# Reordering the head and the late plan of a fused spectral filter and MLP kernel on one Trainium2 core

## The chip, the cores and the metric

The kernel runs on one core of one Trainium2 chip. The metric is the device time of one execution in microseconds (us). For a ratio, the mean time of one kernel's fast runs is divided by the mean time of the other's fast runs of the same rounds, so a ratio is not quite the ratio of the medians that I quote. All runs gave correct results, and all were fast, that is within 1.5% of the fastest run of their kernel, but for one run of the kernel before (614.06 us), which the ratios leave out. The runs were made on at least three chips, and each set of rounds had the kernel before beside it: so ratios are the safer comparison between runs of different rounds. One execution per kernel carries a profile; it can differ from the median by some microseconds, and positions in time ("at 63.68") are microseconds from the start of that profiled execution.

The engines are called by the profile's names: PE is the tensor engine (PEld its weight loads), DVE is VectorE, ACT is ScalarE, POOL is GpSimd, SP is the sync engine; a trailing q means the instruction queue that issues transfers (SPq).

## The reference

```python
X = np.fft.rfft(x, axis=1)                 # x: 8 batches x 3136 tokens x 256
y = np.fft.irfft(X * (filt_r + 1j * filt_i)[None], n=3136, axis=1)
h = y.transpose(0, 2, 1) @ U @ V           # rank 32 along the tokens
u = y + h.transpose(0, 2, 1)
out = u + np.maximum(u @ w_ch1, 0.0) @ w_ch2
```

## The kernel before

3136 is 64 x 49, and the transform is done as matrix products in four stages. Stage 1 transforms 64 points (tile `a` before its trip through DRAM is `asb`), stage 2 transforms 49 points and is followed by the filter product on DVE or POOL (`ta`, `tb`, `y`, or `uv` for batch 0), stage 3 goes back over 49 points (`esb`), stage 4 back over 64 (`ut`). Between stages 1 and 2, and between 3 and 4, the data go out to DRAM (`ct`) and come back in another order: as `a` for stage 2 and as `e` for stage 4. Batch 0 avoids the first trip: its stage 1 is computed already "turned", and PE transposes bring it into order.

The rank-32 part is folded into stage 4. Its 96 contraction rows are 64 rows of `e` plus 32 "H rows" in `e[64:96]`, the same for each residue; the weights' rows `sv[64:96]` hold V. Then come the two MLP products, `mm1` with ReLU and `mm2`. The order of everything is written by hand. One "step" is one eighth of a group of 512 tokens; a batch has 48 to 52 steps of about 1.25 us.

```python
# batch 0: stage 2, filter product, stage 3
turn_a2(0); turn_a2(1)
for j in range(16):
    ...                                     # stage 2 of half tile j into pz
    if j % 5 in (1, 3):                     # product on POOL, from a copy by ACT
        nc.scalar.copy(pc, pz)
        nc.gpsimd.tensor_mul(uv, pc, fin)
    else:                                   # product on DVE
        nc.vector.tensor_mul(uv, pz, fin)
    if half and k + 2 < 8:
        turn_a2(k + 2)                      # 8 transposes, 98 columns each
    if j in (4, 6, 8, 10):
        load_x(1, j // 2 - 2)
    ...                                     # stage 3 and esb copy, four behind

# from batch 0 to the MLP
mid_first()
nc.gpsimd.tensor_copy(sv[64:96, :]..., vnat...)          # V into sv, on POOL
for c in range(3):
    load_e2(0, c)
load_e2(0, 6)
low_rank(0); low_rank_end(0)
for c in (0, 1, 2, 6):
    put_h(0, c)                 # nc.sync.dma_start(t[64:96], h1 ...)
stage4(groups[0], 0); stage4(groups[0], 1)

# the late plan (batches 1 to 7), in steps
lead = 5 if b > 1 else 2        # stage-2 loads ahead of the stage-2 matmul
s = later(s, 1)                 # spacing of stage 2 after a product on DVE
plan_st1(b, later(start[b - 1], -55))                    # stage 1, b > 2
m = later(start[b - 1], -8) if b > 1 else 10             # stage 2
```

A filler group without work (`Group(None, 7)`) stands between batches 0 and 1 and pads the plan there.

## Time and profile before

| | before |
|---|---|
| median of three runs | 607.46 us (605.84 to 607.73) |
| profiled execution | 599.7 us |
| last stage-3 matmul of batch 0 ends | 49.34 |
| first stage-4 matmul of batch 0 | 63.68 |
| first stage-2 matmul of batch 1 | 92.34 |
| first stage-4 matmul of batch 1 | 151.81 |
| from there to the end | 447.89 us |

The positions are read from the timeline, which lists what each engine did in order of time (start, duration, line, what was issued; times count). They cut the program into stretches. This is the sync engine's own timeline of the kernel before, at one of the later changes from batch to batch (start, duration, line, what was issued; times count):

```profile
400.95 0.54 SPq L317 DMA_DIRECT2D ct<-esb  x1
407.05 0.48 SPq L418 DMA_DIRECT2D e<-ct  x1
...
408.27 0.65 SPq L424 DMA_DIRECT2D e<-h  x1
...
409.62 1.43 SPq L308 DMA_DIRECT2D a<-ct  x3
```

The last write of `ct` is issued at 400.95. The load of `e` that reads it can be issued only when it has landed, at 407.05. The three loads of `a` for the next batch do not depend on that write, but they stand behind it in the same queue and go out at 409.62. PE reached the stage-2 matmul before they had landed and waited 2.83 us (the matmul starts at 412.58).

### The profile page before, as it was taken

The page shows a single profiled execution, that of the slowest core. Times are in us where ns is not written, and L with a number is a line of the kernel's source. Part 1 is how long each engine was busy: PE and PEld are TensorE (multiplying, and loading weights), DVE is VectorE, ACT ScalarE, POOL GpSimd, SP SyncE. Part 2 cuts the span into 40 slices and gives each one's busy share as a digit, 9 for nine tenths or more (in the row PEclk, how much of TensorE's full clock was granted, in tenths as well). Part 3 has the DMA queues.
Part 4 walks back from the last instruction along what each step waited for, and adds up shares of the span by engine and source line. Part 5 has one row for each costly group of instructions (what it writes and reads, how often), then busy time and mean ns, then how long its engine had stood idle before and what let it go on. Part 6 is the DMA issues. An engine that isn't in the chain of part 4 may idle for free.

```text
span 599.7 us, 11562 instructions
## 1 busy us (share of the span) xinstructions
PE 525.0 (88%) x4467; PEld 383.4 (64%) x4467; DVE 332.2 (55%) x384; ACT 379.8 (63%) x676; POOL 266.5 (44%) x171
## 2 busy tenths in 40 slices
PE   3992468996799869998999979998999999999997
PEld 2761245674567647775777757775777766777775
DVE  6661645672464646672676357744666367733332
ACT  7362244885377737884786747884886667766663
POOL 4776004992187306860486218830684048600000
PEclk9997677999799999999999989998999999999999
DMA  9997355878447784696558766597364654353212
GB/s 204 145 185 177 54 127 109 241 170 243 118 121 216 156 218 122 184 210 186 151 172 200 171 177 193 148 243 190 117 181 142 173 162 140 100 166 107 89 64 87
DMA packets 82598, 95.32 MB, mean 159 GB/s; under 512 B 6853, under 2 KB 63640, under 8 KB 82544
## 3 DMA queue, kind: packets, MB, share of 16 engines
q1 hardware_dynamic: 74736, 78.40, 45.0%
q0 software_dynamic: 7360, 15.91, 16.3%
q8 instruction: 35, 0.57, 0.4%
q10 hardware_dynamic: 448, 0.28, 0.2%
q14 instruction: 19, 0.16, 0.1%
HBM read 57.42 MB, written 49.77 MB: 179 GB/s over the span
## 4 chain that ended last, share of the span: by engine, by line
PE 54%; DVE 8%; ACT 3%; DMA 3%; issue 2%; SPq 2%; DVEq 0%; ACTq 0%
PE psum L471 19%; PE psum L504 19%; PE psum L340 3%; PE psum L460 3%; PE psum L480 3%; PE psum L332 3%; DVE tb L600 2%; DVE tb L598 2%; DMA a<-ct 2%; PE psum L254 2%; DVE och L512 1%; DVE ta L596 1%; PE psum L396 1%; ACT asb L261 1%; SPq L424 1%
## 5 line engine op out<-in xcount | busy, mean ns | idle before, releaser
L475 ACT ACTIVATE hring<-psum 128x512 f16<-128x512 f32 (+1 forms) x416 | 238.2, 576 | 160.7 <-PE psum L471 158.7
L471 PE MATMUL psum<-ut,w1sb 128*128 128x512 f16 (+1 forms) x832 | 243.6, 375 | 0.5 <-DVE ut L465 0.4
L504 PE MATMUL psum<-w2sb,hring 128*128 128x256 f16 x1536 | 233.7, 276 | 0.0
L602 POOL TENSOR_TENSOR y<-ta,tb 128x1024 f16<-128x1024 f16 x56 | 118.8, 2128 | 221.5 <-DVE tb L600 216.5
L504 PEld LDWEIGHTS <-hring 128*128 128x128 f16 x1536 | 145.1, 99 | 62.3 <-issue 1.9
L465 DVE CAST ut<-psum 128x512 f16<-128x512 f32 x96 | 71.0, 740 | 150.0 <-PE psum L460 135.5
L471 PEld LDWEIGHTS <-w1sb 128*128 128x128 f16 x832 | 103.2, 145 | 22.7 <-issue 6.2
L512 DVE COPY och<-psum 128x512 f32<-128x512 f32 x96 | 66.0, 688 | 50.6 <-PE psum L480 50.5
L314 ACT CAST esb<-psum 98x512 f16<-98x512 f32 x128 | 75.1, 588 | 22.3 <-PE psum L332 17.6
L596 DVE TENSOR_TENSOR ta<-psum,fb 128x1024 f16<-128x1024 f32 x41 | 50.1, 1221 | 35.3 <-PE psum L340 32.0
L460 PEld LDWEIGHTS <-e 96*128 96x128 f16 x768 | 36.8, 100 | 42.6 <-issue 24.0
L340 PE MATMUL psum<-a,w2t 98*128 98x512 f16 x135 | 43.0, 400 | 22.9 <-DMA a<-ct 16.5
L460 PE MATMUL psum<-sv,e 96*128 96x64 f16 x768 | 39.9, 196 | 22.9 <-issue 12.6
L480 PE MATMUL psum<-idn,ut 128*128 128x128 f16 x392 | 54.6, 221 | 0.0
L261 ACT CAST asb<-psum 128x512 f16<-128x512 f32 x78 | 46.0, 591 | 9.3 <-PE psum L254 8.2
L598 DVE TENSOR_TENSOR tb<-psum,fc 64x1024 f16<-64x1024 f32 x41 | 50.2, 1226 | 1.0
L600 DVE TENSOR_TENSOR tb<-psum,fc 64x1024 f16<-64x1024 f32 x41 | 49.9, 1217 | 0.6
L332 PE MATMUL psum<-y,g 128*98 128x512 f16 x105 | 39.8, 379 | 2.7 <-ACT esb L314 1.5
L480 PEld LDWEIGHTS <-ut 128*128 128x128 f16 x392 | 38.9, 99 | 5.2
L254 PE MATMUL psum<-x,wf 128*128 128x256 f16 x168 | 32.4, 284 | 7.8 <-DVE asb L259 6.3
L340 PEld LDWEIGHTS <-w2t 98*128 98x128 f16 x135 | 13.7, 102 | 31.5 <-issue 26.5
L598 POOL TENSOR_TENSOR tb<-pc,fc 64x1024 f16<-64x1024 f16 x15 | 31.9, 2123 | 1.2
(81 smaller groups left out, 341.8 us busy)
## 6 DMA issues: line engine op xcount, KB each, us to landing
out_dram<-och SPq DMA_DIRECT2D x48, 512.0 KB
ct<-esb SPq DMA_DIRECT2D x64, 196.0 KB
x<-in_x_dram POOLq DMA_DIRECT2D x24, 512.0 KB, 7.9
e<-ct SPq DMA_DIRECT2D x48, 256.0 KB
a<-ct SPq DMA_DIRECT2D x56, 196.0 KB
ct<-asb SPq DMA_DIRECT2D x42, 256.0 KB
e<-h SPq DMA_DIRECT2D x24, 128.0 KB
wf<-wf SPq DMA_DIRECT2D x3, 256.0 KB
```

The source lines that it names most:

```text
L314: nc.scalar.copy(esb[b, k][:, 2 * half:2 * half + 2, :].rearrange("p s d -> p (s d)"), pe[0:98])
L340: nc.tensor.matmul(pz, w, a, start=True, stop=True)
L460: nc.tensor.matmul(pu[:, 64 * i:64 * i + 64], e2[b, c][:, i, 128 * dh:128 * dh + 128], sv[:, 64 * r:64 * r + 64], start=(i == 0), stop=Tru ...
L465: nc.vector.tensor_copy(o, v)
L471: nc.tensor.matmul(ph[:, 0:n], w1sb[:, dh, :, t], gr.ut[:, dh, 0:n], start=(dh == 0), stop=(dh == 1))
L475: nc.scalar.activation(h[:, 0:n], ph[:, 0:n], RELU)
L480: nc.tensor.matmul(o[:, dh * 128:dh * 128 + 128], gr.ut[:, dh, t0:t0 + n], idn, start=False, stop=(dh == 1), skip_group_check=True)
L504: nc.tensor.matmul(o, gr.h[tt][:, i * 128:(i + 1) * 128], w2sb[:, tt, :], start=(tt == 0), stop=False, skip_group_check=True)
L512: nc.vector.tensor_copy(gr.och[:, 2 * y:2 * y + 2, :].rearrange("p j d -> p (j d)"), gr.pc)
L598: eng.tensor_mul(tb[0:64], p[64:128], vb[64:128])
L600: eng.tensor_mul(tb[64:128], p[0:64], vb[0:64])
L602: nc.gpsimd.tensor_add(ys[k], ta, tb)
```

## The change

The intent is to shorten the serial head of the program, up to batch 1, and to take the waits for loads out of the later batches. The diff, cut to its core:

```diff
 # x in 2 KB pieces instead of 8 KB
-            t = sb.tile([128, 8, DM], F16, tag="x", bufs=4, name="x")
-            nc.gpsimd.dma_start(t, dram(x.tensor, ..., [[NR * DM, 64], [24 * DM, 2], [1, 8 * DM]]))
+            t = sb.tile([128, 4, XW], F16, tag="x", bufs=4, name="x")
+            for h in range(2):
+                nc.gpsimd.dma_start(t[h:128:2, :, 0:2 * DM],
+                                    dram(x.tensor, ..., [[NR * DM, 64], [2 * DM, 4], [1, 2 * DM]]))
 # batch 0: transposes of 128 columns, four turns ahead of the loop
-                    nc.tensor.transpose(z[0:98, ...], free(fc, 0, 128, ..., [[32, 98]]), idn)
+                    nc.tensor.transpose(z[:, ...], free(fc, 0, 128, ..., [[32, 128]]), idn)
-        turn_a2(0)
-        turn_a2(1)
+        for k in range(4):
+            turn_a2(k)
+        for c in range(4):
+            load_x(1, c)
-            if j % 5 in (1, 3):
+            if j in (4, 6, 9, 11, 14):
-            if half and k + 2 < 8:
-                turn_a2(k + 2)
-            if j in (4, 6, 8, 10):
-                load_x(1, j // 2 - 2)
+            if j < 4:
+                turn_a2(j + 4)
+            if j == 8:
+                nc.scalar.copy(sv[64:96, :]..., vnat...)
 # H rows by VectorE
-        nc.sync.dma_start(t[64:96], free(h1[b], 64, 96, 0, [[0, n], [1, DM]]))
+        nc.vector.tensor_copy(t[64:96], free(h1[b], 64, 96, 0, [[0, n], [1, DM]]))
 # no filler group
-        if b == 0:
-            groups.append(Group(None, 7))
 # from batch 0 to the MLP
     mid_first()
-    nc.gpsimd.tensor_copy(sv[64:96, :]..., vnat...)
-    for c in range(3):
-        load_e2(0, c)
-    load_e2(0, 6)
+    load_e2(0, 0)
+    make_fa(0)
     low_rank(0)
+    first = st1(1)              # 4 of 13 units of batch 1's stage 1
     low_rank_end(0)
+    ...                         # 4 more units, then the other loads of e
 # late plan
-        lead = 5 if b > 1 else 2
+        lead = (2, 6, 9)[min(b, 3) - 1]
-                s = later(s, 1)
+                s = later(s, 2 if b > 1 and k % 2 else 1)
-            plan_st1(b, 13, (0, 1, 3, 4, 7))             # b == 2
+            plan_st1(b, 10, (0, 1, 3, 4, 7))
-            plan_st1(b, later(start[b - 1], -55))        # b > 2
+            plan_st1(b, later(start[b - 1], -60))
-        m = later(start[b - 1], -8) if b > 1 else 10
+        m = later(start[b - 1], -9) if b > 1 else 5
 # batch 1's first stage 4, with no filler group before it, at the end of batch 0's last group
-            if n + 1 < len(groups) and t in (2, 6) and groups[n + 1].c < 7:
+            if n + 1 < len(groups) and t in ((2, 6) if n != 5 else (6, 7)):
```

Not shown: the four parts of batch 1's second filter (`make_fa`) and batch 2's x loads also come one to three steps earlier, and a piece of `fc` is set to zero (the wider transposes read it).

More of the change, by code (lines that the diff above doesn't have):

```diff
@@ L20 @@
 NB = 8
+XW = 2 * DM + 16
 ALPHA, BETA = 1.0 / 64, 1.0 / 49
@@ L141, in bank @@
     def bank(tag):
-        of = {"m": (0, 1), "o": (2, 3), "w": (4,), "e": (7,), "f": (0, 1, 2, 3, 4, 7), "e0": (7, 4), "w1": (7, 5, 6)}[tag]
+        of = {"m": (0, 1), "o": (2, 3), "w": (4,), "e": (7,), "f": (0, 1, 2, 3, 4, 7), "e0": (7, 4), "f0": (0, 1), "w1": (7, 5, 6)}[tag]
         turn[tag] = turn.get(tag, -1) + 1
@@ L163, in load_x @@
         else:
-            t = sb.tile([128, 8, DM], F16, tag="x", bufs=4, name="x")
-            nc.gpsimd.dma_start(t, dram(x.tensor, (b * SEQ + 8 * c) * DM,
-                                        [[NR * DM, 64], [24 * DM, 2], [1, 8 * DM]]))
+            t = sb.tile([128, 4, XW], F16, tag="x", bufs=4, name="x")
+            for h in range(2):
+                nc.gpsimd.dma_start(t[h:128:2, :, 0:2 * DM],
+                                    dram(x.tensor, (b * SEQ + 24 * h + 8 * c) * DM,
+                                         [[NR * DM, 64], [2 * DM, 4], [1, 2 * DM]]))
         xt[b, c] = t
@@ L196 @@
                    free(zero, 32, 64, 0, [[0, NK * DM // 64], [1, 64]]))
+    nc.vector.memset(fc[:, 24:29, :], 0.0)
     usb = hflat[0:64, 0:NR * RANK]
@@ L254, in st1 @@
                     nc.tensor.matmul(pf[:, i * DM:(i + 1) * DM], wf[:, 8 * c + 2 * j + i, :],
-                                     xt[b, c][:, 2 * j + i, :], start=(i == 0), stop=True,
+                                     xt[b, c][:, j, DM * i:DM * i + DM], start=(i == 0), stop=True,
                                      skip_group_check=True)
@@ L290, in turned @@
                         nc.tensor.matmul(z[:, 128 * i:128 * i + 128],
-                                         xt[0, c][:, g + i, 128 * hh:128 * hh + 128],
+                                         xt[0, c][:, (g + i) // 2, DM * (i % 2) + 128 * hh:DM * (i % 2) + 128 * hh + 128],
                                          wf[:, 8 * c + g + i, :], start=(i == 0), stop=True,
@@ L343, in mid_first @@
         a2 = {}
+        spare = [sb.tile([128, 2, 4 * DM], F16, tag="asb", bufs=3, name="asb") for _ in range(3)]
         def turn_a2(k):
-            z = bank("m").bitcast(F16)
+            z = bank("f0").bitcast(F16)
             for i in range(4):
                 for hh in range(2):
-                    nc.tensor.transpose(z[0:98, DM * i + 128 * hh:DM * i + 128 * hh + 128],
-                                        free(fc, 0, 128, 3136 * hh + 4 * k + i, [[32, 98]]), idn)
-            a2[k] = sb.tile([98, 4 * DM], F16, tag="a2", bufs=4, name="a2")
+                    nc.tensor.transpose(z[:, DM * i + 128 * hh:DM * i + 128 * hh + 128],
+                                        free(fc, 0, 128, 3136 * hh + 4 * k + i, [[32, 128]]), idn)
+            if k < 2:
+                a2[k] = sb.tile([98, 4 * DM], F16, tag="a2", bufs=4, name="a2")
+            else:
+                a2[k] = spare[k // 2 - 1][0:98, k % 2, :]
             nc.vector.tensor_copy(a2[k], z[0:98])
@@ L378, in mid_first @@
                 nc.vector.tensor_mul(uv, pz, fin)
-            if half and k + 2 < 8:
-                turn_a2(k + 2)
-            if j in (4, 6, 8, 10):
-                load_x(1, j // 2 - 2)
+            if j < 4:
+                turn_a2(j + 4)
+            if j == 8:
+                nc.scalar.copy(sv[64:96, :].rearrange("p (r q) -> p r q", q=NQ),
+                               vnat.rearrange("p (q r) -> p r q", q=64))
             todo.append((j, uv))
@@ L428, in __init__ @@
             self.b, self.c = b, c
-            self.ntok = {6: 128, 7: 256}.get(c, 512)
+            self.ntok = 512 if c < 6 else 128
             self.h = []
@@ L515, in mm2_part, with make_fa @@
                                        [[NR * DM, 64], [4 * DM, 2], [1, 4 * DM]]), gr.och)
+    fa = fb
+    def make_fa(i):
+        s = slice(8 * i, 8 * i + 8)
+        nc.vector.tensor_copy(fc[0:64, s], fb[64:128, s])
+        nc.vector.tensor_scalar_mul(fc[64:128, s], fb[64:128, s], -1.0)
+        nc.vector.tensor_copy(fa[64:128, s], fb[0:64, s])
+        if i == 3:
+            nc.vector.tensor_copy(fa[64:65, 31, :], fc[0:1, 31, :])
+            for p in (0, 64):
+                nc.vector.memset(fc[p:p + 1, 31, :], 0.0)
     u_hat()
@@ L523 @@
     mid_first()
-    nc.gpsimd.tensor_copy(sv[64:96, :].rearrange("p (r q) -> p r q", q=NQ),
-                          vnat.rearrange("p (q r) -> p r q", q=64))
-    for c in range(3):
-        load_e2(0, c)
+    load_e2(0, 0)
+    make_fa(0)
+    low_rank(0)
+    first = st1(1)
+    for _ in range(4):
+        next(first)
+    low_rank_end(0)
+    for _ in range(4):
+        next(first)
+    load_e2(0, 1)
+    load_e2(0, 2)
     load_e2(0, 6)
-    low_rank(0)
-    low_rank_end(0)
     for c in (0, 1, 2, 6):
@@ L551, in small @@
     def small(s):
-        return s // 8 < len(groups) and groups[s // 8].c >= 6
+        return s // 8 < len(groups) and groups[s // 8].c == 6
     def ok_dve(s):
@@ L564, in at @@
         plan[s].append((f, a))
-    fa = fb
-    def make_fa(i):
-        s = slice(8 * i, 8 * i + 8)
-        nc.vector.tensor_copy(fc[0:64, s], fb[64:128, s])
-        nc.vector.tensor_scalar_mul(fc[64:128, s], fb[64:128, s], -1.0)
-        nc.vector.tensor_copy(fa[64:128, s], fb[0:64, s])
-        if i == 3:
-            nc.vector.tensor_copy(fa[64:65, 31, :], fc[0:1, 31, :])
-            for p in (0, 64):
-                nc.vector.memset(fc[p:p + 1, 31, :], 0.0)
     def plan_mid(b, s, on_pool):
@@ L663, in plan_st1 @@
         return s
-    gens = {}
+    gens = {1: first}
     def step1(b):
@@ L673 @@
         at(8 * c - 14, load_e2, 0, c)
-    for i in range(4):
-        at(i, make_fa, i)
-    for u in range(13):
-        at(3 + u // 3, step1, 1)
+    for i in range(1, 4):
+        at(i - 1, make_fa, i)
+    for u in range(5):
+        at(u // 2, step1, 1)
     for c in range(4):
-        at(9 + 2 * c, load_x, 2, c)
+        at(6 + 2 * c, load_x, 2, c)
     for b in range(1, NB):
         if b == 2:
-            plan_st1(b, 13, (0, 1, 3, 4, 7))
+            plan_st1(b, 10, (0, 1, 3, 4, 7))
         elif b > 2:
-            plan_st1(b, later(start[b - 1], -55))
-        m = later(start[b - 1], -8) if b > 1 else 10
+            plan_st1(b, later(start[b - 1], -60))
+        m = later(start[b - 1], -9) if b > 1 else 5
         z = plan_mid(b, m, (2, 5) if b > 1 else (1, 3, 5))
@@ L693 @@
                 f(*a)
-            if gr.c < 7:
-                mm1(gr, t)
-            if n + 1 < len(groups) and t in (2, 6) and groups[n + 1].c < 7:
-                stage4(groups[n + 1], t // 4)
-            if n and groups[n - 1].c < 7:
+            mm1(gr, t)
+            if n + 1 < len(groups) and t in ((2, 6) if n != 5 else (6, 7)):
+                stage4(groups[n + 1], t // 4 if n != 5 else t - 6)
+            if n:
                 mm2_part(groups[n - 1], t)
```

## The prediction

The sum of 36.4 us is the estimate from times in the trace of the kernel before, such as the 184 and 104 ns of the weight loads, the 0.69 us of L570, the 2.5 us of the loads of `a` and the clock of 0.77.

> **What bounds the kernel now.** I read the page's busy shares and slices first, to see where the tensor engine (PE) is not full; then its waits; then the timeline at the longest.
>
> ```profile
> span 599.7 us, 11562 instructions
> PE 525.0 (88%) x4467; PEld 383.4 (64%) x4467; DVE 332.2 (55%) x384; ACT 379.8 (63%) x676; POOL 266.5 (44%) x171
> ...
> PE   3992468996799869998999979998999999999997
> ...
> PEclk9997677999799999999999989998999999999999
> ```
>
> PE is busy 525.0 of 599.7 us and no other engine passes 63%, so the kernel is PE work plus 74.7 us of PE holes plus a slower clock. A slice is 15 us: the holes sit in the first eleven slices, and there PEclk falls to 6 or 7 tenths. By stretches (the windows view, with the end of each hole from the timeline) the idle time is 10.4 us in 0-15, 1.2 in 15-45, 14.3 in 45-63.7, 22.3 in 63.7-165 and 26.5 after.
>
> The waits of PE, longest first:
>
> ```profile
> PE psum L340 <- DMA a<-ct: 16.5, 6, 5.5
> PE psum L460 <- issue: 12.6, 1, 12.6
> PE psum L236 <- DVE hring L231: 9.1, 1, 9.1
> PE psum L254 <- DVE asb L259: 6.3, 1, 6.3
> PE psum L340 <- DVE tb L600: 5.8, 11, 1.1
> PE psum L460 <- DMA e<-h: 5.4, 1, 5.4
> PE psum L460 <- DMA a<-ct: 3.1, 1, 3.1
> ```
>
> Columns are total us, number, longest. All but the third (start of the program) and the fifth (DVE product) are hand-overs from one stage to the next through DRAM, or DVE work in front of one. The one put down to "issue" is no issue cost. The timeline of 45.6 to 64 shows it:
>
> ```profile
> 50.80 0.27 PE L404 MATMUL psum<-hp,kr 128*96 128x256 f16 x1 [0.47 <-ACT hp L399]
> 51.11 0.36 ACT L406 CAST h<-psum 32x256 f16<-32x256 f32 x1 [0.36 <-PE psum L404]
> 52.85 1.74 SPq L418 DMA_DIRECT2D e<-ct  x3
> ...
> 55.27 2.94 SPq L424 DMA_DIRECT2D e<-h  x3
> ...
> 63.68 0.53 PE L460 MATMUL psum<-sv,e 96*128 96x64 f16 x7 [12.61 <-issue]
> ```
>
> PE stops at 51.07. Three tile loads and then, behind them in the same queue, the three copies of the H rows are issued; the tokens' MLP starts at 63.68.
>
> The groups by form, up to 64 us:
>
> ```profile
> L378 DVE TENSOR_TENSOR uv<-psum,fb 128x1024 f16<-128x1024 f32 x10 | 12.1, 1223 | 4.5 <-PE psum L340 3.3 <-DMA x<-in_x_dram 1.0 <-DMA fb<-in_filt_i_dram 0.2
> L349 PEld LDWEIGHTS <-fc 128*98 128x98 f16 x64 | 11.8, 259 | 2.0 <-issue 0.9 <-ACT fc L301 0.4 <-DVE fc L299 0.2
> ...
> L290 PEld LDWEIGHTS <-x 128*128 128x128 f16 x48 | 5.0, 147 | 1.3 <-DMA x<-in_x_dram 1.1
> ```
>
> A load of 98 weight columns occupies 11.8/64 = 184 ns; one of 128 columns occupies 5.0/48 = 104 ns.
>
> [...] granted clock 0.73, 0.70, 0.76, 0.79 over 45-105, where the holes are, and 1.00 on either side. [...] The stage-2 loads of batch 1 are issued from 89.85 and their matmul runs at 92.34: 2.5 us for 196 KB[...]. [...] L570, 64x2048, took 0.69 us. So an H-row copy (32x2048) should also take 0.69.
>
> **The change, part by part.**
>
> *Batch 0's filter product.* Weights of the 64 transposes go from 98 to 128 columns: 64 x (184 - 104) = 5.1 us less PE. Four turns run before the loop, the rest in its first four steps; DVE takes 11 products for 10, ACT 5 copies for 6. Before, turns to stage 3 ran 20.37 to 49.34 = 29.0 us with PE nearly full; after, PE needs 24. DVE needs 8 x 0.69 + 11 x 1.22 = 19.0 from about 22, so 41 plus the last stage 3. Both give an end near 44.5, **4.8 us earlier**. The 2 KB pieces double the x issues; at 0.66 us each that is 24 x 0.7 = 17 us more on POOL (44% busy): free. On x's arrival I put zero.
>
> *H rows by DVE, batch 1's stage 1 ahead.* From end of stage 3 to the first stage 4 was 14.3 us. After: esb copy 0.6, its write landed (49.97 to 52.85) 2.9, one e load about 3.5 (estimate: 2.5 for 196 KB, here 256 KB beside writes) = 7.0 to 7.5; DVE's copies (3 x 0.69 + 0.2 = 2.3) lie beside it. Stage 4 starts at 44.5 + 7.5 = 52 instead of 63.68: **6.9 us** more, with eight of thirteen stage-1 units done in the hole. H copies then cost DVE 8 x 2.3 = 18 us in all, on an engine at 55%.
>
> *Into batch 1's stage 2.* Before: from stage 4 (63.68) to the stage-2 matmul (92.34) 28.7 us, of which 6.3 was PE behind the twelve DVE copies that build the second filter (each 0.69), and 5.5 the load of a. After, five units remain. DVE chain: ut copies done 2.5, three filter copies, asb, three, asb: 8.2. Two ct writes and the last small one: about 14 (before, the small one's matmul at 83.40 to the load's issue at 89.85: 6.5). Load: 16.5. So the wait for a **does not go**: PE reaches the stage-2 matmul about 8 us after stage 4 and waits 8. But it is 12 us sooner after stage 4; it then has 5 fewer MLP steps behind it, at about 0.85 us of PE each 4. Net **8.2 us**.
>
> *The gap group between batches 0 and 1.* Batch 1's filter must now end at its step 41 of 48, not 45 of 52. Before, PE waited 5.4 us for e<-h, then ran at clock 0.77 (150-165). After: last e write to first use needs about 5.2 + 3.5 = 8.7 us, there are six steps of about 1.08 us = 6.5, so 2 to 3 us of wait remain. **3 us, plus 1.5 of clock.**
>
> *More lead for the loads.* After 165 us, PE waits 10.5 + 3.1 us for a<-ct, longest 3.1. The lead grows from 5 steps to 9 (batch 2: 6); 4 x 1.25 us = 5 exceeds every one. 80% of 13.6 = 11. Wider spacing of stage 2 should take half of the 4.9 us behind L600, 2.5. Against it, DVE's 18 us of H copies in the same stretches: I charge 2.5. **11 us.** Clock there goes from 0.98 to about 1 in 300-500: 1 us.
>
> Sum: 4.8 + 6.9 + 8.2 + 4.5 + 11 + 1 = 36.4. From 607.5: **571**, rounded to 570.
>
> **The rivals.**
>
> *A: DVE becomes the engine that others wait for.* The H copies come at a batch's end, in program order before products and evacuations; a copy that waits for its row blocks ut copies behind it. For: L600 waits already number 11. Against: 55% busy, and a copy is shorter than a product (1.22). It would eat all of the 11: 582.
>
> *B: the head's gain is taken back at batch 1.* The chain stage 1, write, load remains serial, and without the gap group nothing pads batch 1's end. If both waits grow by 5 us with the slow clock after them: 583.
>
> *C: everything lands.* If the wait for a is half of mine because DVE is freed sooner, and late waits all vanish: 556.
>
> *D: 2 KB pieces hurt.* DMA is at 91 to 102% over 0-45. [...] 3 to 5 us in the head, once: 574. [...]
>
> **Range and chances.** The head terms (20 us) rest on visible serial chains and I trust them to 5 us; the late 11 could be 0 or 15. A and B together give about 590, C 556. Range 555 to 587. Same needs two thirds of the sum to vanish. Faster 0.95, same 0.04, slower 0.01.
>
> **What would show it.** Right: transposes' weight loads near 104 ns; the first stage-4 matmul at 50-54; no 6 us wait on an asb copy; a wait of 5 to 10 us for a at batch 1; 2 to 4 us at the first stage 4 of batch 1; after it almost nothing on a<-ct; PE busy about 510, its clock low for some 25 us instead of 60. Wrong: weight loads still 184; stage 4 later than 57; a new row of waits on L465 or H copies adding over 8 us; a<-ct still above 6 us late. If the late waits stay, the time is 580 or more; if the wait for a at batch 1 is gone too, below 560.

## The result and the profile after

The changed kernel takes 578.0 us in the median of four runs (577.55 to 579.73), the kernel before 607.6 us (605.84 to 608.88) in the same rounds. The ratio is 0.952, with a 95% interval of 0.949 to 0.955. The gain is 29.6 us, and the prediction said 37.

The profiled executions differ by less than that, 599.7 against 575.8 us in span: the profiled execution of before took 601.8 us, 5.8 under that median, and the one of after 577.55, 0.5 under. The table below therefore explains 23.9 us. Where the other 5.7 lie in the timed runs no profile tells; the mean clock was 0.962 in the profiled execution of before, and 0.937 to 0.963 in the runs of that kernel that the later rounds list, so lower clock may be part of it.

These are the page's first line, its busy shares, and its slices (of 14.4 us) for the kernel after:

```profile
span 575.8 us, 11582 instructions
...
PE 511.0 (89%) x4467; PEld 374.5 (65%) x4467; DVE 352.3 (61%) x418; ACT 386.2 (67%) x676; POOL 275.3 (48%) x193
...
PE   2866459987899999999999999999998899999996
...
PEclk9997779999999999999999999999999999999999
```

PE is busy for 511.0 us, 14 less than before with as many matmuls; the clock is low in three slices only. The holes of the first six slices are still there. From the twelfth slice on, nearly all is full.

The stretches, with the prediction's terms for each:

| stretch (us) | before | after | difference | predicted |
|---|---|---|---|---|
| start to the end of batch 0's stage 3 | 49.34 | 56.77 | +7.4 | -4.8 |
| to the first stage 4 | 14.34 | 10.28 | -4.1 | -6.9 |
| to the first stage 4 of batch 1 | 88.13 | 76.78 | -11.4 | -8.2 and -3 |
| to the end | 447.89 | 431.97 | -15.9 | -1.5, -11 and -1 |

The first row has the wrong sign. The third is almost exact. The last is larger than its sum, and is made differently: in that stretch PE was busy for 419.88 us before and 412.12 after, with about as many matmuls in the records (3697 and 3713), at a mean clock of 0.98 and 1.00. So 7.8 of its 15.9 us are shorter busy time, and only 8.2 are shorter idle time.

The waits of PE over the whole program say where to look (total us, number, longest):

```profile
PE psum L345 <- DVE tb L614: 10.7, 11, 1.5
PE psum L241 <- DVE hring L236: 8.8, 1, 8.8
PE psum L469 <- DMA e<-ct: 6.6, 2, 4.5
PE psum L345 <- DMA a<-ct: 6.5, 1, 6.5
PE psum L337 <- ACT esb L319: 5.7, 1, 5.7
PE psum L337 <- POOL uv L386: 3.8, 3, 2.5
```

Against before: the wait called "issue" (12.6) and the one for `e<-h` are gone, the wait for `a` is down from 16.5 us in six waits to one of 6.5. In place of the first stand 6.6 us for `e<-ct`, of them 4.5 at the first stage 4 of batch 0 and 2.05 at that of batch 1. New is a single wait of 5.7 us on ACT's `esb` copy, and the wait on DVE's `tb` product has almost doubled. The timeline from 39 us on shows the first:

```profile
39.56 6.91 ACT L393 COPY sv<-hring 32x3136 f16<-32x3136 f16 x1
...
47.12 1.01 PE L337 MATMUL psum<-uv,g 128*98 128x512 f16 x2 [5.71 <-ACT esb L319]
...
50.53 2.36 DVE L389 TENSOR_TENSOR uv<-psum,fb 128x1024 f16<-128x1024 f32 x2 [7.85 <-PE psum L345]
...
63.16 0.47 SPq L430 DMA_DIRECT2D e<-ct  x1
...
67.05 0.59 PE L469 MATMUL psum<-sv,e 96*128 96x64 f16 x8 [4.53 <-DMA e<-ct]
```

The copy of V into `sv`, which POOL did before with nothing behind it, now stands in ACT's program in the middle of the loop and takes 6.91 us there. ACT also evacuates stage 3. PE waits 5.71 us for that, and then DVE 7.85 for PE. Between 42 and 50 us PE was busy for 2.88 us, and the clock granted to it was 0.58. The last two rows are the other end of the chain: 5.7 us pass between the end of the last `esb` copy (57.44) and the issue of the load of `e`, where before it was 2.9.

The groups by form up to 62 us show the part that did go as planned, and its cost elsewhere:

```profile
L389 DVE TENSOR_TENSOR uv<-psum,fb 128x1024 f16<-128x1024 f32 x11 | 13.3, 1219 | 12.5 <-PE psum L345 11.7 <-PE psum L342 0.7
...
L355 PEld LDWEIGHTS <-fc 128*128 128x128 f16 x64 | 6.1, 157 | 2.0 <-issue 0.7 <-ACT fc L306 0.4 <-DVE fc L304 0.3
```

A transpose's weight load went from 184 to 6.1/64 = 95 ns. But DVE's products now have 12.5 us of idle time in front of them, nearly all for PE, where before it was 4.5.

### The profile page after: what moved, and what is told of

The parts are those of the page before. It is cut to its first block, busy times and chain, and to the rows that moved or that the text cites. A ratio compares the mean times of both kernels' runs of the same rounds, so it can differ in the third digit from the quotient of the medians.

```text
span 575.8 us, 11582 instructions
## 1 busy us (share of the span) xinstructions
PE 511.0 (89%) x4467; PEld 374.5 (65%) x4467; DVE 352.3 (61%) x418; ACT 386.2 (67%) x676; POOL 275.3 (48%) x193
## 3 DMA queue, kind: packets, MB, share of 16 engines
q0 software_dynamic: 16960, 15.91, 18.7%
## 4 chain that ended last, share of the span: by engine, by line
PE 63%; DVE 8%; ACT 2%; issue 1%; ACTq 0%; DVEq 0%
PE psum L513 23%; PE psum L480 23%; PE psum L345 3%; PE psum L337 3%; PE psum L489 3%; PE psum L469 3%; DVE tb L614 2%; PE psum L259 2%; DVE ut L474 1%; DVE tb L612 1%; DVE ta L610 1%; PE psum L408 1%; ACT hring L484 1%; DVE och L521 1%; ACT pc L620 1%
## 5 line engine op out<-in xcount | busy, mean ns | idle before, releaser
L513 PE MATMUL psum<-w2sb,hring 128*128 128x256 f16 x1536 | 230.5, 273 | 0.0
L513 PEld LDWEIGHTS <-hring 128*128 128x128 f16 x1536 | 143.2, 98 | 63.0 <-issue 3.2
L345 PE MATMUL psum<-a,w2t 98*128 98x512 f16 x113 | 34.8, 384 | 17.6 <-DVE tb L614 10.7
L610 POOL TENSOR_TENSOR ta<-pc,fb 128x1024 f16<-128x1024 f16 x15 | 32.0, 2134 | 5.2 <-ACT pc L620 5.2
```

Of the source, the lines that this page charges most:

```text
L513: nc.tensor.matmul(o, gr.h[tt][:, i * 128:(i + 1) * 128], w2sb[:, tt, :], start=(tt == 0), stop=False, skip_group_check=True)
L610: eng.tensor_mul(ta, p, va)
```

## The experiments

Twelve kernels ran. The edits are against the changed kernel unless another is named. "Rest" is the time from the first stage-4 matmul of batch 1 to the end of the profiled execution; "head" is the position of the first stage-4 matmul of batch 0.

| kernel | median us | ratio to before (95%) | stage 3 ends | head | rest |
|---|---|---|---|---|---|
| before | 607.6 | 1 | 49.34 | 63.68 | 447.89 |
| after | 578.0 | 0.952 (0.949 to 0.955) | 56.77 | 67.05 | 431.97 |
| e1_sv_pool | 577.26 | 0.949 (0.944 to 0.954) | 51.56 | 64.11 | 431.95 |
| e2_x3bufs | 579.22 | 0.951 (0.946 to 0.956) | 59.94 | 67.27 | 432.02 |
| e3_h_dma | 591.54 | 0.973 (0.969 to 0.977) | 59.02 | 75.88 | 437.97 |
| e4_x8k | 573.64 | 0.943 (0.939 to 0.948) | 53.47 | 63.75 | 432.09 |
| e5_x8k_svcut | 576.49 | 0.946 (0.943 to 0.949) | 53.17 | 65.05 | 432.09 |
| e6_lead_old | 580.46 | 0.953 (0.951 to 0.955) | 58.24 | 68.46 | 431.95 |
| e7_space_old | 575.85 | 0.945 (0.942 to 0.947) | 58.12 | 68.41 | 428.45 |
| e8_before_hdve | 601.11 | 0.986 (0.980 to 0.992) | 50.22 | 57.76 | 451.26 |
| e9_lead_space_old | 580.33 | 0.956 (0.952 to 0.961) | 56.95 | 67.36 | 432.93 |
| e10_best | 561.82 | 0.924 (0.921 to 0.927) | 45.00 | 53.45 | 428.68 |
| e11_best_w98 | 565.61 | 0.932 (0.929 to 0.936) | 51.12 | 58.45 | 430.25 |
| e12_late_old | 601.12 | 0.985 (0.979 to 0.992) | 57.49 | 68.25 | 450.48 |

Two things make this table readable. The rest is the same to 0.2 us in the six kernels that have the changed late plan, or only its lead set back, and that keep H on DVE (431.95 to 432.09), so it measures the late plan without the noise of the head. The head, on the other hand, moves by up to 1.4 us between single profiles of kernels that are equal up to there (after, e6, e7, e9, e12: 67.05 to 68.46). Two profiles are not typical of their kernel: that of e11 is the slowest of its six runs (570.56 against a median of 565.61), that of e5 the fastest of its four (573.54 against 576.49).

### e1: the V copy back on POOL

```diff
-            if j == 8:
-                nc.scalar.copy(sv[64:96, :]..., vnat...)
...
     mid_first()
+    nc.gpsimd.tensor_copy(sv[64:96, :]..., vnat...)
```

> Theory (the SV copy sits in the path): in the changed kernel ScalarE spends 6.91 us on the copy of V into sv (39.56 to 46.47) in the middle of batch 0's loop; PE waits 5.7 us for an esb copy behind it, VectorE 7.9 and GpSimd 7.7. With that copy back on GpSimd after the loop (as in the kernel before), nothing waits for it: the loop ends 6 to 7 us earlier, the first stage 4 starts at about 60 instead of 67.05, and the whole run takes 570 to 572 us. Rival (the loop is held by something else, the GpSimd products that start only at 36.13, or the filters' arrival, so the ScalarE copy only fills a hole): the loop ends less than 2 us earlier and the run takes 576 or more.

Stage 3 ended 5.2 us earlier, at 51.56, and PE's 5.7 us wait for `esb` was gone. But the first stage 4 came only 2.9 us earlier, and the time, for which I had expected 570 to 572, is not separable from the changed kernel's. The timeline of this run shows what took the gain:

```profile
50.54 7.26 POOL L542 COPY sv<-hring 32x3136 f16<-32x3136 f16 x1
...
51.04 7.33 DVE L528 TENSOR_SCALAR fc<-fb 64x2048 f16<-64x2048 f16 x1
...
60.46 0.37 PE L413 MATMUL psum<-hp,kr 128*96 128x256 f16 x1 [5.71 <-DVE asb L264]
```

The DVE instruction in the second row takes 0.69 us elsewhere. Here it was begun 0.5 us after POOL's copy and ended 0.57 us after it, and PE then waited 5.71 us for the DVE work behind. What held it is not in the trace, which shows only that it took 7.33 us for 0.69 beside POOL's 7.26 us copy, and ended with it. In the kernel before the same POOL copy ran from 47.49 to 54.39 with none of the filter copies beside it: they came after stage 4 there. The changed kernel moved one of them, `make_fa(0)`, into just this stretch. So both homes of the V copy in it are bad ones: in ACT's loop PE waits 5.71 us behind it, and after the loop on POOL a DVE instruction beside it takes 7.33 us for 0.69.

### e2: three x buffers instead of four

```diff
-            t = sb.tile([128, 4, XW], F16, tag="x", bufs=4, name="x")
+            t = sb.tile([128, 4, XW], F16, tag="x", bufs=3, name="x")
```

> Theory (a load that starts too soon): in the changed kernel GpSimd, free of the SV copy, issues batch 2's first x piece at 55.63, just as batch 0's last rows are written; the first e load is issued 5.1 us after the last write instead of 2.9, and lands at 67.05. With three x buffers instead of four, that load has to wait until PE has read batch 1's first piece (about 60), so the e load should go out about 2 us earlier, and the run take about 576. Rival (the write's landing has nothing to do with x): the gap of 5.1 us stays, and the run is the same within 0.5 us, or slower by the tighter x buffers later.

The question was the 5.7 us between the last `esb` copy and the load of `e`. In the changed kernel, POOL issues an x load of batch 2 (512 KB, at 55.63) just as the last `ct` writes are on their way. With three buffers that load waits until 63.44, and the 5.7 us shrank to 2.4 (60.62 to 63.04). In e1, where the x loads came at 57.74, it was 2.6. In both cases the write queue had 0.20 MB left to move in that time, and beside it ran 0.69 MB of x in the changed kernel and nothing in e2. So in these runs the last write took about twice as long to land with a large load beside it, 5.7 us against 2.4 and 2.6. The time did not improve, as the fewer buffers also made batch 1's x loads later, POOL waited for them, and stage 3 ended at 59.94; I had expected 576.

### e3: H rows by DMA again

```diff
-        nc.vector.tensor_copy(t[64:96], free(h1[b], 64, 96, 0, [[0, n], [1, DM]]))
+        nc.sync.dma_start(t[64:96], free(h1[b], 64, 96, 0, [[0, n], [1, DM]]))
```

> The H rows written by DMA again, as in the kernel before. Theory (moving them to VectorE helps at the hand-overs): the first stage 4 starts later by about 3 us (three more DMAs on the same queue behind the e load), the first stage 4 of batch 1 by 2 to 3, and the run takes 581 to 584. Rival (the copies on VectorE are what doubled the wait of stage 2 for VectorE's products, 4.9 us before and 10.7 after): that wait falls back to about 5, the hand-overs lose little, and the run takes 574 or less.

This costs 13.5 us, where I had expected 3 to 6. PE waits 25.2 us in eight waits for `e<-h`, the longest 11.1 us at the first stage 4, which comes at 75.88: the H copies stand in the sync queue behind four writes of stage 1 and the loads of `e`. The rest grows by 6 us. The wait on `tb` falls from 10.7 to 4.7 us, so DVE's H copies do weigh on the products (or PE, waiting elsewhere, comes later to them; this run cannot separate the two), but far less than the transfers would. The opposite edit, e8 below, points the same way.

### e4: x in 8 KB pieces again

```diff
-            t = sb.tile([128, 4, XW], F16, tag="x", bufs=4, name="x")
-            for h in range(2):
-                nc.gpsimd.dma_start(t[h:128:2, :, 0:2 * DM], ...)
+            t = sb.tile([128, 8, DM], F16, tag="x", bufs=4, name="x")
+            nc.gpsimd.dma_start(t, dram(x.tensor, ..., [[NR * DM, 64], [24 * DM, 2], [1, 8 * DM]]))
```

> x in pieces of 8 KB again, one DMA of 128 partitions for each chunk. Theory (piece size hardly matters, as predicted: zero): the run is within 1.5 us of 578. Rival A [...]: the run is slower by 2 us or more, and x lands later than the 6.9 us median. Rival B (more descriptors and issues hurt the head: the first x matmuls end at 21.8 instead of 20.1): the head is 1.5 us earlier and GpSimd's products start at about 33 instead of 36, so the run is 2 us faster or more.

This is Rival B, and my prediction of zero was wrong. It is 4.4 us faster, with intervals of the ratio that do not overlap (0.939 to 0.948 against 0.949 to 0.955), and all of it is in the head; the rest is 432.09. Two things differ there. The turned stage 1 of batch 0 ended at 19.69 instead of 21.80. And POOL was free for its first filter product earlier, as the POOL timelines of the changed kernel and of this run show, in this order:

```profile
31.05 3.75 POOL L168 DMA_DIRECT2D x<-in_x_dram  x6
...
36.13 4.20 POOL L386 TENSOR_TENSOR uv<-pc,fb 128x1024 f16<-128x1024 f16 x2
```

```profile
29.50 1.83 POOL L167 DMA_DIRECT2D x<-in_x_dram  x3
...
31.62 4.51 POOL L384 TENSOR_TENSOR uv<-pc,fb 128x1024 f16<-128x1024 f16 x2
```

Six issues take 3.75 us and three take 1.83, and the products that stand behind them start 4.5 us later: 1.9 us of that is these issues, 1.6 is that they began later, and most of the rest is POOL waiting for a load before its last issue. How the 4.4 us divide between this and the earlier end of stage 1 was not tested. The small pieces are twice as many issues (and 16960 packets instead of 7360 in q0 of the page, the only queue whose count differs) on an engine that had something waiting just then. What the packets alone cost was not tested.

### e5: 8 KB pieces, and the V copy in seven parts

```diff
-            if j == 8:
-                nc.scalar.copy(sv[64:96, :]..., vnat...)
+            if 8 <= j < 15:
+                r = slice(7 * (j - 8), 7 * (j - 8) + 7)
+                nc.scalar.copy(sv[64:96, :]...[:, r], vnat...[:, r])
```

> 8 KB pieces of x as in e4_x8k, and the SV copy stays on ScalarE but is cut into seven pieces of about 1 us, one in each of steps 8 to 14 of batch 0's loop. Theory (the 6.9 us block in ScalarE's order is what the loop waits for; the first sv experiment lost its gain only because the GpSimd copy and VectorE's filter copies hold each other up): PE's 5.7 us wait for an esb copy goes, no VectorE copy is stretched to 7 us, and the run takes 567 to 569 against 573.6 for e4_x8k. Rival (ScalarE's total in the loop is the limit, so pieces cost as much as the block): 572 or more.

No gain over e4, where I had expected 5 to 7 us: 576.49 us, ratio intervals overlapping, stage 3 ending at 53.17 instead of 53.47 even in the fastest of its runs. The seven parts took 1.13 to 1.17 us each, 8.1 us together, and ACT was busy for 10.4 of the 12 us from 30 to 42 and for 7.8 of the 8 from 42 to 50. Cut up or not, the copy does not fit beside the evacuations that ACT has in that loop. It must leave the loop.

### e6, e7, e9: lead and spacing set back, alone and together

```diff
 # e6 and e9
-        lead = (2, 6, 9)[min(b, 3) - 1]
+        lead = 5 if b > 1 else 2
 # e7 and e9
-                s = later(s, 2 if b > 1 and k % 2 else 1)
+                s = later(s, 1)
```

> The changed kernel with the old lead of the stage-2 loads (2 steps for batch 1, 5 for the others), all else kept. Theory (the lead is what removed the 13.6 us of waits for a<-ct after batch 1): 8 to 12 us of these waits come back, the run takes 585 to 590. Rival (stage 1 being planned 5 steps earlier, at -60 instead of -55, was enough, since the loads wait for its writes): waits for a<-ct stay under 3 us and the run is within 2 us of 578.

> The changed kernel with the old spacing of stage 2 (one step after each product, not two after every odd one). Theory (VectorE carries H copies among its products now, so a tighter spacing makes PE wait longer for the products): the wait for tb grows from 10.7 to 13 us or more and the run is 2 to 4 us slower. Rival (the new spacing itself moved stage 2 to where VectorE is late, and is why 4.9 became 10.7): the wait falls to 5 to 7 us and the run is 3 to 5 us faster.

> The changed kernel with both the old lead and the old spacing; either alone left the waits for a<-ct after batch 1 at zero to 1.2 us. Theory (order in the sync engine's queue: the stage-2 loads of the next batch were stuck behind an e load that waits for the last ct write; either the lead or the spacing, which puts off the e load by four steps, brings them in front of it): with both old the loads are planned at step -14 and the e load at -16, so the load is behind again: 7 to 12 us of waits for a<-ct come back after batch 1 and the stretch after batch 1's first stage 4 takes 437 us or more, against 432.0 in the changed kernel, 431.95 with the old lead and 428.45 with the old spacing. Rival (what removed the waits is that stage 1 is written 5 steps earlier, or that the H rows are no longer DMAs in that queue): they stay away, and the stretch takes 428.5.

With the old lead alone, the rest is 431.95 and the time is that of the changed kernel: the longer lead removed nothing by itself. With the old spacing alone the rest is 428.45, 3.5 us shorter, and the ratio intervals do not overlap those of the changed kernel. The waits of PE after 165 us in e7, where the changed kernel has 10.7 us in 11 waits, the longest 1.5:

```profile
PE psum L345 <- DVE tb L614: 5.5, 10, 1.1
```

So the wider spacing, which I had credited with halving that wait, doubled it. With both set back (e9) the rest is 432.93: on the old spacing the longer lead is worth 4.5 us (432.93 - 428.45), and 3.7 us of waits for `a` are back, the longest 1.4. That is far from the 13.6 us that the kernel before had after 165 us (10.5 at stage 2, 3.1 at stage 4), so most of those had another cause. I had expected at least 437 here, and that missed.

### e8: the kernel before with H rows by DVE

```diff
-        nc.sync.dma_start(t[64:96], free(h1[b], 64, 96, 0, [[0, n], [1, DM]]))
+        nc.vector.tensor_copy(t[64:96], free(h1[b], 64, 96, 0, [[0, n], [1, DM]]))
```

> The kernel before with only one part of the change: the H rows written by VectorE instead of by DMA. Undoing this part in the changed kernel cost 13.5 us. Theory (it is worth about as much alone: the two waits at hand-overs, 12.6 and 5.4 us, shrink by 3 to 5 us each and the wait of 4.6 us for e<-h late in the run goes; VectorE's products then are late as in the changed kernel): 598 to 602. Rival (its worth comes from the other parts, which leave less room for the rows, so alone it brings nothing): 605 or more.

The head gains 5.9 us (57.76 against 63.68), and the time 8 us of medians, a ratio of 0.986. From the end of stage 3 to the first stage 4 are 7.5 us instead of 14.3, which is what the prediction gave for that step with stage 1 moved as well. After 165 us PE still waits 11.9 us for `a` at stage 2 (10.5 before). So the H copies ahead of the stage-2 loads in the sync queue were not what made those loads late; the 3.1 us for `a` at a stage 4 are gone, with 1.1 us for `e<-ct` in their place. The waits for `tb` grow from 4.9 to 8.0 us after 165 us, and the rest from 447.89 to 451.26: in the late part of these two profiles H by DVE costs more than it brings.

### e12: the whole late plan of before in the changed kernel

```diff
 # e9, and
-            plan_st1(b, 10, (0, 1, 3, 4, 7))
+            plan_st1(b, 13, (0, 1, 3, 4, 7))
-            plan_st1(b, later(start[b - 1], -60))
+            plan_st1(b, later(start[b - 1], -55))
-        m = later(start[b - 1], -9) if b > 1 else 5
+        m = later(start[b - 1], -8) if b > 1 else 5
```

> The changed kernel with the whole late plan of the kernel before (old lead, old spacing, and stage 1 and stage 2 of each later batch planned from the old steps: stage 1 at 55 steps ahead of its batch instead of 60, stage 2 at 8 instead of 9), but with the H rows still written by VectorE and no filler group. It asks where the other 10 us of waits for a behind the loads from ct went. If the earlier planning of stage 1 and stage 2 removed them: after 165 us PE waits for a<-ct again at 8 us or more, and the time from batch 1's first stage 4 to the end is 436 us or more (432.9 with old lead and old spacing alone). If the removal of the H-row DMAs from the same queue did it: a<-ct stays at 3 to 5 us and that stretch at 431 to 434 us. Speed: 580 to 588 in the first case, 578 to 582 in the second.

This was the last run, and it shows that the three plan numbers that it sets back beyond e9 carry the late gain. That came out larger than I had expected: 601.12 us, 20.8 us more than e9 (on another chip, but the ratios to before say the same: 0.985 and 0.956), with a rest of 450.48 instead of 432.93. The waits of PE after 165 us:

```profile
PE psum L345 <- DMA a<-ct: 10.0, 4, 3.2
PE psum L345 <- DVE tb L614: 8.4, 15, 1.1
```

The 10.0 us for `a` are back, nearly the 10.5 of the kernel before. The sync engine's timeline shows how, at the same batch change in e12 and then in e9:

```profile
330.52 0.87 SPq L279 DMA_DIRECT2D ct<-al  x1
...
333.94 0.52 SPq L322 DMA_DIRECT2D ct<-esb  x1
339.75 0.47 SPq L430 DMA_DIRECT2D e<-ct  x1
...
340.95 1.38 SPq L313 DMA_DIRECT2D a<-ct  x3
```

```profile
320.20 0.52 SPq L322 DMA_DIRECT2D ct<-esb  x1
323.59 0.47 SPq L430 DMA_DIRECT2D e<-ct  x1
...
324.76 1.43 SPq L313 DMA_DIRECT2D a<-ct  x3
```

In both, the loads of `a` are stuck behind a load of `e` that waits for the last `ct` write. In e12 that wait is 5.3 us long (339.75 less 333.94 + 0.52), in e9 2.9 us (323.59 less 320.20 + 0.52). What differs in the traces is what runs beside that write: in e12 the end of stage 1 (`ct<-al`) and the x loads of the next batch come 3.4 us before it; in e9, with stage 1 planned five steps earlier, they came 12.7 us before it, at 307.5. The 16 DMA engines were 74% busy during the wait in e12 and 40% in e9. PE then waited 2.33 us for `a` at that place in e12, and 0.68 in e9.

The waits for `a` are 6.3 us of the 17.6 by which the rest grew, and those for `tb` 2.9. Nearly all that remains is longer busy time. The windows view for the rest, of e12 and then of e9, gives the stretch, its length, the busy time and number of instructions of PE, PEld, DVE, ACT and POOL, the clock, the busy share of the DMA engines and GB/s:

```profile
149.02:599.50 450.48, 421.93 (x3717) 310.28 (x3717) 267.02 (x311) 301.92 (x554) 194.00 (x112) 0.98 0.56 151
144.67:577.60 432.93, 414.19 (x3713) 307.68 (x3713) 263.43 (x308) 300.61 (x551) 193.02 (x111) 1.00 0.58 157
```

PE is busy 7.7 us longer for about as many matmuls, at the lower clock. Part of that comes right after the waits. In e12, those for `a` that end at 276.74, 344.96 and 410.01 (3.24, 2.33 and 2.43 us) are each followed, within 0.4 us, by 3.4 us in which the granted clock was 0.50; in the kernel before, two waits of 2.8 us are followed in the same way within 1.3 us. By an estimate from these figures, 3.4 us at half the clock cost 1.7 us, so that such a wait costs more than itself. It does not always happen: a wait of 2.99 us before and two of 1.96 (one in each kernel) were not followed by it. In e9, with no wait for `a` over 1.4 us, it never happens after 165 us. Which of the three numbers in this edit does it (stage 1 of batch 2, stage 1 of the later ones, stage 2) was not separated.

### e10 and e11: what the experiments point to

```diff
 # e10: e4's x, e7's spacing, and
     for a in range(0, NK, 8):
         load_filters(a, a + 8)
+        if a == 0:
+            nc.gpsimd.dma_start(vnat, moe_V)       # V after the first filter part
...
-            if j == 8:
-                nc.scalar.copy(sv[64:96, :]..., vnat...)
...
+    nc.scalar.copy(sv[64:96, :]..., vnat...)       # ahead of the loop
     mid_first()
     load_e2(0, 0)
+    nc.gpsimd.tensor_copy(gate, e2[0, 0][0:1, 0, 0:2])   # holds POOL's x loads back
 # e11: e10 with transposes of 98 columns
-                    nc.tensor.transpose(z[:, ...], free(fc, 0, 128, ..., [[32, 128]]), idn)
+                    nc.tensor.transpose(z[0:98, ...], free(fc, 0, 128, ..., [[32, 98]]), idn)
```

> What the runs so far point to, together: x in 8 KB pieces, old spacing, V loaded after the first filter chunk and copied into sv by ScalarE before batch 0's loop, where ScalarE is idle for 9 us, and batch 2's first x load held back until batch 0's first e tile has landed (GpSimd reads two elements of it first). Theory (three separate costs of the change: SV copy about 5.5 us, early x load about 3, spacing 3.5): batch 0's stage 3 ends at about 48 instead of 53.5 (e4_x8k), the e load is issued about 2.6 us after the last esb copy instead of 6, the first stage 4 starts at 54 to 56, the stretch after batch 1's first stage 4 takes 428.5, and the run takes 560 to 563. Rival (the filters or x arrive too late for the faster loop, V's earlier load makes that worse): stage 3 ends at 51 or later and the run takes 567 or more.

> e10_best with the transposes' weights at 98 columns again, as in the kernel before. Theory [...]: their weight loads take 184 ns instead of about 100, PE has 5 us more in batch 0's product, of which about half is on the path because VectorE needs 19 us there too; 2 to 3 us slower than e10_best. Rival (the loop is bound by VectorE and by the filters' arrival): same within 0.7 us.

e10 takes 561.82 us in the median of six runs (559.68 to 562.81), 16 us less than the changed kernel and 7.6% less than the kernel before in the mean of the same rounds. The V copy now lies here, in e10's timeline:

```profile
20.53 7.24 ACT L541 COPY sv<-hring 32x3136 f16<-32x3136 f16 x1 [0.80 <-DMA hring<-in_moe_V_dram]
```

It still takes ACT 7.24 us, but DVE does the copies of the transposes then and nothing waits for ACT. Stage 3 ends at 45.00, where the prediction had put it for the changed kernel (44.5), and the first stage 4 runs at 53.45 (52). Between 42 and 50 us the clock is 1.00. The gate did less than meant: from the last `esb` copy to the load of `e` are 4.3 us (45.67 to 49.94), less than 5.7, more than e2's 2.4, with no x load beside it; in e11 it was 2.4. The DMA view shows a backlog: from 34 to 42 us the transfers issued by POOL, batch 1's x at their end, took 95% of the DMA engines' time and the `ct` writes 11%, and from 44 to 48 us these writes took 99%. So 0.79 MB of them were still to move in the 4.3 us of e10, against 0.20 MB, one write, in e11 and e2, where the loop ended later. No run tests what shifting batch 1's x would bring.

e11 is 3.8 us slower than e10 (2 to 3 expected), with ratio intervals that do not overlap. The transposes' weight loads occupied 11.7 us in e11's profile and 5.0 in e10's. The full-width weight loads are therefore worth having, though not all of the 3.8 us need be their own time: in e11's profile PE ran at a clock of 0.50 from 22 to 30 us, in e10's at 1.00. That profile is of the slowest of e11's six runs, so whether the others had this low clock is not known.

## Why the prediction was right or wrong

The time fell inside the range, 8 us above the point. That is partly luck: in the profiles the first term has the wrong sign, 12 us from what was told, and the stretch after batch 1's first stage 4 gained more than its sum for another reason than the one told. The prediction's own sign "stage 4 later than 57" for being wrong came true, at 67.05. Step by step:

*Transposes.* Right as a cost: 95 ns each, where near 104 was foretold. Their place in the sum was not reached in the changed kernel, because something else filled the loop.

*Batch 0's filter product, "an end near 44.5".* Wrong: 56.77. This is the step that failed. The sum of DVE and PE work in it was sound, as e10 shows with 45.00, but it left out one line of the diff, the V copy that moved from POOL into ACT's stream at step 8 of the loop. It took 6.91 us there, with 5.7 us of PE waiting and a clock of 0.58 from 42 to 50 us. Taking it away brought the end 5.2 us forward (e1), and with 8 KB pieces of x and V loaded earlier 8.5 us (e10 against e4). I had counted what each engine does in the loop for DVE, PE and ACT's product copies, and not this copy at all.

*"On x's arrival I put zero", POOL's issues "free".* Wrong: worth 4.4 us against the change (e4). Rival D had the sign and the size (3 to 5 us in the head), but did not name POOL; the turned stage 1 did end 2.1 us later, and POOL's products began 4.5 us later. The issues were set against POOL's average of 44% busy, instead of against what POOL does at that place, where filter products stood behind them.

*H rows by VectorE and stage 1 ahead, "52 instead of 63.68".* The step from stage 3 to stage 4 gained 4.1 us of 6.9. H by DVE is confirmed as the large part (e3: 13.5 us in all; e8: alone, it brings this step to the 7.5 us that were told). The missing 2.8 us are the landing of the last write, which I took as 2.9 us from the kernel before and which took 5.7 beside an x load that the freed POOL issued early (e2); the load of `e` then took 3.9 us to its first use (3.5 told).

*Into batch 1's stage 2, and the gap group.* Right, and by their steps: stage 2 came 15.7 us after stage 4 (16.5 foretold), with a wait for `a` of 6.5 us (8 foretold); the wait at batch 1's first stage 4 was 2.05 us at 143.83 (2 to 3 foretold). Together the stretch gained 11.4 us where 11.2 was the sum of the two terms.

*More lead for the loads, "4 x 1.25 us = 5 exceeds every one".* Half right. No wait for `a` is left after 165 us, and the rest shortened by 15.9 us where 13.5 was the sum. But the idle time shrank by 8.2 us and not by 11, since the waits for `tb` grew by 5.8, and the busy time shrank by 7.8, where the terms for the clock were 1.5 and 1. The prediction's own figures held more than that: 0.02 of 200 us (0.98 in 300-500) is 4 us, and 0.23 of 15 us (150-165) is 3.4. The reason was wrong as well. The lead alone brings nothing (e6), and with the other spacing it brings 4.5 us (e9 against e7). Of the 10.0 us at stage 2 that are there in e12, 6.3 went because stage 1 and stage 2 of each batch were planned earlier (e12 against e9), a line of the diff that I had read only as making room for the lead, and 3.7 by the lead or the spacing (e9); the 3.1 at a stage 4 went with the H copies in the queue (e8). *Wider spacing "should take half of the 4.9 us"*: wrong in sign; those waits doubled, and the spacing cost 3.5 us (e7).

*Clock.* PE busy is 511.0 (about 510 foretold). The clock was low in three slices, 43 us rather than 25, from the loop that had failed to the wait for `a` at batch 1. Waits of 2.3 to 3.2 us were followed by half the clock five times after 165 us (before and e12), and one of 2.99 was not: here the length of a wait alone did not decide it.

*Rival A* came true only in small: H copies took 0.69 us each, 18 us in all as worked out, and in the changed kernel no wait is put down to them, but the products behind them come later (`tb` after 165 us: 4.9 to 8.0 in e8, with nothing else changed). In the changed kernel with the old spacing (e7) that is no more than 5.5, so there it costs little, and most of the 10.7 is the spacing's. *Rival B* did not: the stretch up to batch 1's first stage 4 gained what was told. *Rival C* (556) needed everything to land; with the faults found here mended, the time comes near it (561.82).

## What to carry to other kernels

Account for every line of a diff that puts work on an engine, and set it against what that engine has to do in that stretch, not against its average share: one copy of 7 us was harmless on an idle engine (e10), made PE wait 5.71 us in ACT's loop, and on POOL had a DVE instruction of 0.69 us beside it take 7.33 us (e1). It was no cheaper on either engine: 6.90 and 7.26 us on POOL (before, e1), 6.91 and 7.24 on ACT (after, e10). Where issues share a queue, as in SPq here, ask what the entry ahead of a load waits for: in e12 the three loads of `a` went out only after an issue of `e` that waited 5.3 us for a write, and a longer lead brought nothing alone (e6) and 4.5 us on the old spacing (e9 against e7); planning the work of each batch earlier, which among other things moved other traffic away from that write, helped here far more (17.6 us of the rest, e12 against e9). A freed engine can start its transfers earlier, as POOL did here (x at 55.63), so look at what those transfers will then run beside: from the end of the last `esb` copy, or from the issue of the last write, to the issue of the load of `e` that waited for it, 2.4 to 2.9 us passed in e2, e11 and e9 (DMA engines 40% busy in e9), 5.3 to 5.7 us beside 512 KB loads of x in e12 and the changed kernel (74% in e12), and 4.3 us behind a backlog of earlier writes in e10. And when waits shrink, look at the busy time too: here half of the late gain, 7.8 of 15.9 us, was shorter busy time, at a clock of 1.00 instead of 0.98.
